# A 33rd head of zeros, one copy of 594 columns for each key and query tile, and a new instruction list

## The chip, the cores and the metric

The kernel runs on one core of one Trainium2 chip. The metric is the device time of one execution in microseconds; a profiled execution also gives a trace, whose span runs from the first to the last instruction. The engines are named as the profile names them: PE (TensorE, matmul), DVE (VectorE), ACT (ScalarE), POOL (GpSimd), and SP, whose queue issues nearly all DMAs.

## What is computed

One transformer block over 2048 tokens of width 576 with 32 heads of 18, and a feed-forward layer of width 4608. Its first half is a linear attention whose feature map is a pair of softmaxes:

```python
h = layernorm(x) * (1 + ca) + sa             # ca, sa: from silu(c) @ w_mod
q, k, v = split(h @ wqkv)                    # 32 heads of 18
pq, pk = q @ w_phi, k @ w_phi                # per head, 18 x 18
phi_q = concat(softmax(pq), softmax(-pq))    # 36 features per head
phi_k = concat(softmax(pk), softmax(-pk))
o = phi_q @ (phi_k^T v) / (phi_q @ sum(phi_k) + 1e-6)
x = x + ga * (o @ wo)
h = layernorm(x) * (1 + cb) + sb
x = x + gb * (relu(h @ w1) @ w2)
```

## The kernel before

**Tiling.** The 2048 tokens are 16 tiles of 128 rows, four tiles to a block. Channels are five chunks (KC = 5) of 128, 128, 128, 128 and 64 rows. The weights of keys and queries are folded with w_phi and with the modulation ahead of use (`wfold`), so that one projection gives the feature inputs of a tile. A projection of a tile is ten matmuls: five chunks for each of two PSUM banks. Heads lie in groups of three (GH = 3, GF = 54 columns); 32 heads make ten full groups and one of two heads, and the buffers have room for eleven full groups (DP = 594). Before the change a key or query tile fills 270 columns of the first bank and 306 of the second (`PARTS`), and leaves PSUM in two copies (`features`): 540 columns for the ten full groups and 36 for the two heads of the last. POOL has set the missing head's columns to zero beforehand (`pad_keys`, `queries_out`).

**Order.** Everything up to the second block of the feed-forward layer is written out by hand as a list of steps (`order`), and each engine runs its instructions strictly in the order of that list; POOL's alone are placed by the framework. The steps that matter here, a number after the name being the tile, pair or chunk:

- LP, LK, LA, LV, LQ, WOL, LW, W2: DMAs of x, key weights, modulation weights, value weights, turned query weights, wo, w1 and w2.
- LS (statistics of one tile of x), RS (its reciprocal deviation, on ACT, for two tiles), LX (normalise two tiles, on DVE), PT and PX (turn two tiles on PE and copy them out) or LT (turn one by DMA).
- WT (turn a chunk of the key weights on PE), WTE (copy it out), F1 and F0 (fold a chunk of keys or queries with w_phi), FA and FB (copy out its two banks).
- SIL (silu of c), MC1.0 and MC1.1 (shift and scale on PE), MSH and MSC (copy them out), SC1, SCv, SC0 (scale the folded weights), Bv, B1, B0 (their bias rows on PE), BEv, BE1, BE0 (copy these out).
- V, K, Q (project a tile), VE, KE, QE (copy it out).
- MN, LO, MX, HI, EX, SU, SA, RC, SC: the softmaxes of the keys (smallest and largest, subtract, exp, sums on PE, their copy, reciprocal, scale); SD takes the sums on DVE instead of SU and SA. The same with q in front is for two tiles of queries; qT turns them by DMA.
- KVa to KVc (keys times values on PE), KVE (copy out), NU and NUE (attention of the first two tiles and its division), OT and OTE, WS (scale wo by its gate on DVE), WO and WOE (output projection, residual), then S2, R2, X2, PN, PNE (second norm) and G.0, the first group of the feed-forward layer.

A last 1 moves a step from its usual engine to the other: KE, VE and QE are on ACT unless so marked, LS, WTE, FA, FB, PX, SC, BE and KVE are on DVE unless so marked. Tiles of PSUM for folds, projections and turned weights come from one pool of three (`mm_tile`), so a step that opens a tile waits until the third one before it has been copied out.

**Statistics.** On DVE a tile takes two `bn_stats` and a `bn_aggr` (L234, L235). On ACT (L228 to L230) it takes two passes over the tile with a running sum; what these passes write out is not used, and goes to `junk`.

**The buffer `room`.** Several short-lived tensors share one buffer of 12760 columns and are told apart by columns alone. `part(o, k, n)` gives k times n columns from column o:

```python
wv_raw, wqT, wq_plain = part(0, KC, D), part(3552, NGR, D), part(7008, KC, D)
junk = room[:, 9944:9944 + D]
```

So `wq_plain`, the folded query weights, ends at column 7008 + 5 x 576 = 9888. `zero_rows` lets POOL set the unused lower 64 partitions of the fifth chunk to zero in `wk_plain`, `wv_raw`, `wfold[1]`, `wv_sb`, then in `v`, then in `wq_plain` and `wfold[0]`. The framework makes an instruction wait for earlier ones that touch the same bytes of a buffer.

Of the kernel before, what the change touches and what calls it, by code (L numbers as in the profile page):

```python
# [44 lines left out]
def kernel(  # L45
# [41 lines left out]
    def copy(eng, dst, src):  # L87
        if eng is A_:
            A_.activation(out=dst, in_=src, func=ACT.Copy)  # L89
        else:  # L90
            eng.tensor_copy(out=dst, in_=src)
# [254 lines left out]
    def fold(which, ci):  # L346
        ps = pool_tiles["F", which, ci] = mm_tile("ps_fold")
        for g in range(NGR):
            nf = G6 if g < 5 else 2 * DH
            T_.matmul(ps[0:KK[ci], g // 4, (g % 4) * G6:(g % 4) * G6 + nf], lhsT=wT[which][0:G6, g, ci * P:ci * P + KK[ci]],  # L350
                      rhs=wbd[0:G6, g, 0:nf], start=True, stop=True)
# [93 lines left out]
    def proj(pss, lhs, w, splits):  # L445

        for ps, (cs, cn) in zip(pss, splits):
            for ci in range(KC):
                T_.matmul(ps[:, 0:cn], lhsT=lhs[:, ci, :], rhs=w[:, ci, cs:cs + cn],  # L449
                          start=(ci == 0), stop=(ci == KC - 1))  # L450
# [479 lines left out]
    LX.2 K.0 LS.8 PM.3 PM.0 K.2 LS.11 KE.2.1 VE.1 RS.3 KE.0 LQ.4 K.1 LX.3 LQ.0 LS.10.1 KE.1 LQ.3 K.3 KE.3 F0.4  # L930
    FB0.4.1 FA0.4.1 LT.5 V.5 LS.9 RS.4 LT.4 F0.2 VE.5 K.5 MN.0 FA0.2.1 FB0.2.1 F0.1 LO.1 KE.5 FB0.1.1 LT.6 RS.5
    FA0.1 CR LX.4 SC0.4 LT.7 V.4 VE.4 LP4.6 LX.5 F0.0 FB0.0.1 FA0.0.1 SC0.1 MX.0 SC0.2.1 K.6 KE.6 F0.3 FB0.3.1
    FA0.3.1 K.4 KE.4 LT.10 K.7 B0 LS.13 KE.7 BE0.1.1 LS.12.1 K.10 SC0.0 KE.10 RS.6 LT.9 LT.8 BE0.0 SC0.3 Q.1
    HI.1 Q.2 LS.14.1 QE.2 Q.0 LO.0 LM.1 LM.0 LT.11 HI.0 QE.1.1 V.9 QE.0 LS.15.1 VE.9 K.9 LM.2 KE.9 EX.0 Q.3 Q.7
    QE.3 RS.7 V.7 VE.7 MN.1 qMX.0 MX.1 qHI.0 LX.6 SU.0 EX.1 QE.7.1 LO.2 K.8 KE.8 K.11 KE.11 LT.12 LT.13 HI.2
    SU.1 LX.7 EX.2 qMN.0 qLO.0 K.12 KE.12 LO.3 SA.1 RC.1 qEX.0 RW.1 HI.3 RW.0 RWE.0.1 V.8 RWE.1 V.13 SA.0 LT.14
    VE.8 RC.0 LT.15 K.15 RC2.0 K.14 VE.13 qEX.1 MN.2 KE.15 MX.2 W1 KE.14 qSU.0 K.13 EX.3 RC2.1 LW.2.1 KE.13 Q.4
    QE.4 SU.3 V.15 LW.1.0 Q.8 LO.5 SC.0 qSA.0 HI.5 LO.4 RC2.2 HI.4 EX.4 LW.1.1 SC.1 SA.3 RC.3 VE.15 LW.0.0 qRC.0
    V.6 MN.3 QE.8 MX.3 SU.2 RD.2 RD.0 LW.0.1 LO.7 VE.6 SA.2 EX.5 SU.4 Q.14 SA.4 HI.7 SC.3 RC.2 SC.2 Q.13 V.14
# [5 lines left out]
    RL.4 W2.1.1 G.2 FW.7 qMN.2 qT.1 NV.0 qLO.2 qHI.2 NVE.0 RL.6 Y.1.0.0 RL.7 Y.1.1.0 qEX.4 Y.1.1.1 qEX.5 qSD.5
    qSD.4 FW.8 NV.1 qRC.2 OU.0 Y.1.0.1 RL.8 NVE.1 qSC.2 WP.0 Y.0.0.0 WPE.0 S3.0 W2.2.1 Y.1.0.2 YE.1.0 OU.1 WP.1
    WPE.1 S3.1 Y.1.1.2 YE.1.1 R3 X3 XT qT.2 MD.0 MD.3 Y.0.0.1 Y.0.0.2 Y.0.1.0 MD.1 MD.2 Y.0.1.1 YE.0.0 MD.4
    Y.0.1.2 YE.0.1
# [104 lines left out]
```

## Time and profile before

| what | us |
|---|---|
| median of 3 runs (414.61 to 415.11) | 415.0 |
| the profiled execution's own time | 417.61 |
| its span | 415.4 |
| first projection of a tile starts at | 18.04 |
| last keys times values start at | 88.70 |
| feed-forward layer (G.0) starts at | 103.79 |

The profile's groups give the busy time of a kind of instruction, its mean length in ns, and the idle time of its engine just ahead of it with what ended that idle time. A timeline row has the start, the length of the stretch, the engine, the line, the output and inputs with their shapes, a count, and in square brackets the idle time before it. An engine starts an instruction before the one ahead has left it, so rows can overlap, and the distance between starts is what an instruction costs its engine.

### The profile page before, as it was taken

What the parts mean: (1) busy time and instruction counts of PE and PEld (TensorE: products, weight loads), DVE (VectorE), ACT (ScalarE), POOL (GpSimd) and SP (SyncE); (2) the same over time, 40 slices, a digit from 0 to 9 for tenths busy, and PEclk for the clock granted to TensorE, in tenths of its full rate; (3) what the DMA queues carried; (4) which work ended last, traced back from release to release, by engine and by line L of the source; (5) the groups of instructions that cost most, each with busy time, mean ns of one, the idle gap of its engine ahead of it and who ended that gap; (6) DMA issues with size and microseconds to landing.
All of it is one profiled execution on the core that took longest, in us unless ns stands there. A gap on an engine that the chain in (4) does not pass through costs nothing.

```text
span 415.4 us, 9230 instructions
## 1 busy us (share of the span) xinstructions
PE 405.5 (98%) x3955; PEld 330.0 (79%) x3955; DVE 235.2 (57%) x597; ACT 182.7 (44%) x310; POOL 11.6 (3%) x39
## 2 busy tenths in 40 slices
PE   6999999989999999999999999999999999999996
PEld 4677777777888788788878888888888888878876
DVE  6789999977768564637345552846292532330011
ACT  7898999944761064016302630452055014302500
POOL 8010000000000000000000000000000000000000
PEclk9899999999999999999999999999999999999999
DMA  8955937489543520502051014104210502010000
GB/s 239 254 88 143 250 50 232 58 227 390 203 87 101 120 45 2 115 16 33 15 102 32 17 33 85 46 2 74 58 34 2 117 24 25 16 32 16 2 2 28
DMA packets 72163, 35.44 MB, mean 85 GB/s; under 512 B 56689, under 2 KB 69754, under 8 KB 72122
## 3 DMA queue, kind: packets, MB, share of 16 engines
q1 hardware_dynamic: 71520, 34.83, 35.3%
q8 instruction: 31, 0.51, 0.5%
q10 hardware_dynamic: 602, 0.02, 0.1%
q14 instruction: 10, 0.08, 0.1%
HBM read 19.27 MB, written 2.37 MB: 52 GB/s over the span
## 4 chain that ended last, share of the span: by engine, by line
PE 78%; DVE 12%; ACT 4%; DMA 2%; issue 2%; SPq 1%; DVEq 0%; ACTq 0%
PE ps_y L860 34%; PE ps_h L817 31%; PE ps_h L809 4%; PE ps_wo L725 3%; DVE tree L468 2%; PE ps_wo L449 2%; DVE tree L466 1%; DMA wo_sb<-in_A_wo_dram 1%; DVE xn L243 1%; DVE phik L481 1%; DMA wk_raw<-in_A_wqkv_dram 1%; DVE phik L479 1%; DVE phik L539 1%; ACT v L89 1%; PE ps_num L668 1%
## 5 line engine op out<-in xcount | busy, mean ns | idle before, releaser
L822 ACT ACTIVATE H<-ps_h 128x1024 bf16<-128x1024 f32 x72 | 73.5, 1022 | 170.8 <-PE ps_h L809 122.3
L860 PE MATMUL ps_y<-w_sb,H 128*128 128x288 bf16 (+2 forms) x1188 | 143.0, 282 | 0.0
L860 PEld LDWEIGHTS <-H 128*128 128x128 bf16 x1188 | 113.7, 98 | 27.3
L817 PE MATMUL ps_h<-hT,w1a 128*128 128x256 bf16 x640 | 74.9, 273 | 0.2 <-DVE hT L419 0.2
L817 PEld LDWEIGHTS <-w1a 128*128 128x128 bf16 x640 | 61.3, 98 | 9.6 <-issue 2.1
L868 DVE TENSOR_TENSOR outt<-ps_y,row_gb 128x288 bf16<-128x288 f32 (+2 forms) x33 | 14.8, 449 | 86.4 <-PE ps_y L860 86.2
L817 PE MATMUL ps_h<-hT,w1b 128*128 128x256 bf16 x512 | 59.2, 273 | 0.0
L449 PEld LDWEIGHTS <-hT 128*128 128x128 bf16 x480 | 46.0, 97 | 13.0 <-issue 0.9
L817 PEld LDWEIGHTS <-w1b 128*128 128x128 bf16 x512 | 49.8, 98 | 6.8 <-issue 0.8
L730 DVE TENSOR_TENSOR x_sb<-x_sb,ps_wo 128x288 bf16<-128x288 bf16 x28 | 12.6, 454 | 31.3 <-PE ps_wo L725 24.8
L243 DVE TENSOR_SCALAR xn<-x_sb,mv,rstd 128x576 bf16<-128x576 bf16 x32 | 12.5, 432 | 20.1 <-ACT rstd L239 20.1
L449 PE MATMUL ps_q<-wfold,hT 128*128 128x270 bf16 (+1 forms) x160 | 21.5, 285 | 0.1
L449 PE MATMUL ps_v<-wv_sb,hT 128*128 128x288 bf16 x160 | 21.2, 286 | 0.2 <-ACT phik L89 0.2
L449 PE MATMUL ps_k<-wfold,hT 128*128 128x270 bf16 (+1 forms) x160 | 21.3, 285 | 0.0
L526 DVE TENSOR_REDUCE ln_s<-room 128x66 f32<-128x1188 bf16 x14 | 19.0, 1367 | 2.6 <-ACT room L508 2.6
L809 PE MATMUL ps_h<-hT,w1c 64*128 64x256 bf16 x288 | 19.9, 271 | 0.0
L234 DVE BATCH_NORM_STATS2 bst<-x_sb 128x6 f32<-128x288 bf16 x48 | 19.4, 447 | 0.0
L508 ACT ACTIVATE room<-room 128x1188 bf16<-128x1188 bf16 x16 | 18.8, 1186 | 0.8 <-DVE room L479 0.3
L508 ACT ACTIVATE phik<-phik 128x2376 bf16<-128x2376 bf16 x8 | 17.5, 2193 | 0.3 <-DVE phik L481 0.2
L809 PEld LDWEIGHTS <-w1c 64*128 64x128 bf16 x288 | 12.1, 94 | 5.2 <-issue 3.8
L468 DVE TENSOR_TENSOR tree<-tree 128x264 bf16<-128x264 bf16 (+2 forms) x48 | 14.6, 305 | 1.7
L419 DVE TENSOR_SCALAR hT<-hT,mod 128x256 bf16<-128x256 bf16 x35 | 9.7, 344 | 6.2 <-DMA hT<-xn 6.2
(155 smaller groups left out, 362.1 us busy)
## 6 DMA issues: line engine op xcount, KB each, us to landing
w_sb<-in_B_w_dram SPq DMA_DIRECT2D x6, 864.0 KB, 10.5
...
```

Source lines behind the costliest of these rows:

```text
L234: V.bn_stats(out=st[:, half, :], in_=x_sb[:, t0 + j, half * 288:(half + 1) * 288])
L243: V.tensor_scalar(out=xn[:, j, 0:D], in0=x_sb[:, t0 + j, :], scalar1=mv[:, j, 0:1], scalar2=rs[:, j:j + 1], op0=ALU.add if j in minus else ...
L449: T_.matmul(ps[:, 0:cn], lhsT=lhs[:, ci, :], rhs=w[:, ci, cs:cs + cn], start=(ci == 0), stop=(ci == KC - 1))
L468: V.tensor_tensor(out=a[:, :, 0:w], in0=a[:, :, 0:w], in1=a[:, :, w:2 * w], op=op)
L508: A_.activation(out=E[:, j:j + k], in_=E[:, j:j + k], func=ACT.Exp)
L526: V.tensor_reduce(out=t["l", b][:, k * 22:(k + 1) * 22].rearrange("p (g s) h -> p g s h", s=2), op=ALU.add, axis=mybir.AxisListType.X, in_ ...
L730: V.tensor_tensor(out=xs[:, cs:cs + cn], in0=xs[:, cs:cs + cn], in1=p[:, 0:cn], op=ALU.add)
L809: T_.matmul(f1[q][:, e, hh * w:hh * w + w], lhsT=w1["c"][r, 2 * q + hh, :], rhs=hT[r, 4, :], start=(first and hh == 0), stop=(not first an ...
L817: T_.matmul(f1[q][:, e, hh * w:hh * w + w], lhsT=w1_at(2 * q + hh, e, ci), rhs=hT[:, ci, :], start=(first and hh == 0 and ci == 0), stop=( ...
L822: A_.activation(out=p2t["H1"].rearrange("p (e j) n -> p e j n", e=2)[:, :, 2 * q:2 * q + 2], in_=f1[q][:].rearrange("p e (h n) -> p e h n" ...
L860: T_.matmul(ps[:, 0, 0:cn], lhsT=p2t["H1"][:, k, j * P:(j + 1) * P], rhs=p2t["w2"][:, k, c], start=(k == 0), stop=(k == NJ - 1))
L868: V.tensor_tensor(out=o[:, c], in0=ps[:, 0, 0:cn], in1=rows["gb"][:, c], op=ALU.mult)
```

## The change

1. `wfold`, `wk_plain` and `wq_plain` get 594 columns instead of 576. The last group of the fold has three heads, the third of them made of zeros (`feature_maps`, `fold`).
2. A key or query tile fills 297 columns at the end of the first bank and 297 at the start of the second, which lie side by side, and leaves PSUM in one copy of 594 columns. The zeros of the missing head come out of the projection, and POOL no longer writes them.
3. The list of steps is a new one. In it ACT takes the statistics of five tiles (0, 1, 5, 14, 15) instead of eight (2, 3, 1, 6, 10, 12, 14, 15), and steps change place and engine throughout.

```diff
-    wfold = {i: wqp.tile([P, KC, D], BF16, name=f"wfold{i}") for i in (0, 1)}
+    wfold = {i: wqp.tile([P, KC, DP], BF16, name=f"wfold{i}") for i in (0, 1)}
...
-    wv_raw, wqT, wq_plain = part(0, KC, D), part(3552, NGR, D), part(7008, KC, D)
+    wv_raw, wqT, wq_plain = part(0, KC, D), part(3552, NGR, D), part(7008, KC, DP)
...
-    wplain = {1: p0.tile([P, KC, D], BF16, name="wk_plain"), 0: wq_plain}
+    wplain = {1: p0.tile([P, KC, DP], BF16, name="wk_plain"), 0: wq_plain}
...
-        for g, c, h, nh in ((slice(0, 5), 0, 0, 3), (slice(0, 5), GF, 3, 3), (slice(5, 6), 0, 0, 2)):
+        for g, c, h, nh in ((slice(0, 5), 0, 0, 3), (slice(0, 5), GF, 3, 3), (slice(5, 6), 0, 0, 3)):
...
-            nf = G6 if g < 5 else 2 * DH
+            nf = G6 if g < 5 else GF
...
-        c0, n = ((0, 432), (432, 144))[half]
+        c0, n = ((0, 432), (432, DP - 432))[half]
...
+    PH = DP // 2
+    PARTS = [(0, PH), (PH, PH)]
...
-    PARTS = [(0, 5 * GF), (5 * GF, D - 5 * GF)]
...
     def pad_keys(b):
-        G.memset(phik_g(b)[:, :, NG - 1, 0:GF], 0.0)
         G.memset(phik[b][:, TPB * NG * DW:], 0.0)
...
-        proj((ps[:, 0], ps[:, 1]), hT1[b][:, :, j * P:(j + 1) * P], w, HALVES if name == "v" else PARTS)
+        proj((ps[:, 0], ps[:, 1]) if name == "v" else (ps[:, 0, 512 - PH:], ps[:, 1]), hT1[b][:, :, j * P:(j + 1) * P], w, HALVES if name == "v" else PARTS)
...
     def features(dst, ps, eng):
-        copy(eng, dst[:, 0:10, :].rearrange("p (a g) c -> p a g c", a=2),
-             ps[:, :, 0:5 * GF].rearrange("p a (g c) -> p a g c", c=GF))
-        copy(eng, dst[:, 10, :].rearrange("p (f h) -> p f h", h=GH)[:, :, 0:2],
-             ps[:, 1, 5 * GF:5 * GF + 36].rearrange("p (f h) -> p f h", h=2))
+        copy(eng, dst, ps[:].rearrange("p a n -> p (a n)")[:, 512 - PH:512 + PH].rearrange("p (g c) -> p g c", c=GF))
...
     def queries_out(t, eng):
         b, j = t // TPB, t % TPB
-        if b not in pq_zero:
-            pq_zero.add(b)
-            G.memset(pq[b][:, :, NG - 1, :], 0.0)
...
     order = """
-    LP.1 LH WBD LS.3.1 LK.2 WT.4 WTE.4 LK.0 WT.0 LK.1 LS.2.1 WTE.0 WT.1 WTE.1 F1.4 FB1.4 LP.0 LS.0 Z.11 RS.1
-    LX.1 FA1.4.1 F1.1 Z.8 LA.1 SIL WT.3 WTE.3 WT.2 LA.0 LS.1.1 Z.3 FB1.1.1 FA1.1.1 F1.0 RS.0 WTE.2.1 FB1.0 FA1.0
-    PT.1 LX.0 F1.3 F1.2 FA1.3 PX.1.1.1 MC1.0 PX.1.0.1 FB1.3.1 MSH LV MC1.1 FB1.2 MSC SCv.3 SCv.0 PT.0 PX.0.1
...
-    RC.6 SC.5 SU.7 Q.10 QE.10 KVa qT.0 SA.7 SC.6 WOL RC.7 SC.7 WS.1 VE.12 KVb KVc Q.12 KVE.0.1 RD.1 KVE.1 NU.1
+    LH LP.0 LS.0.1 LP.1 LK.1 WT.3 LS.3 LS.1.1 LS.2 LK.0 WBD WTE.3 Z.6 WT.0 WTE.0 WT.2 RS.1 LX.1 WT.1 WTE.1
+    WTE.2.1 F1.0 FA1.0 LK.2 LA.0 SIL RS.0 FB1.0.1 WT.4 LA.1 PT.1 PX.1.1 F1.1 WTE.4.1 FA1.1 FB1.1 LV LP4.2
+    PX.1.0.1 F1.2 MC1.0 FA1.2.1 FB1.2.1 CR F1.3 FA1.3.1 LX.0 LQ.2 F1.4 FB1.4 MC1.1 MSH MSC SCv.0 SCv.1 FA1.4.1
+    FB1.3.1 SCv.3 PT.0 SCv.2.1 Bv PX.0.1.1 PX.0.0 BEv.1.1 BEv.0.1 B1 BE1.1.1 SC1.0.1 BE1.0.1 LQ.3 LQ.4 LP4.4
...
+    qMX.1 WOL LW.1.0 RC.3 RC.2 HI.5 VE.4 LO.7 HI.7 RD.0 qSU.0 qSA.0 SC.1 V.15 SC.2 MCE2 LO.6 HI.6 QE.12 V.11
...
+    SC.4 SU.6 SA.6 RC.6 VE.14 SC.5 SU.7 SA.7 SC.6 KVa KVb RC.7 SC.7 KVc WS.1 KVE.0.1 Q.4 QE.4 KVE.1 WS.0 NU.1
+    NUE.1 Q.6 NU.0 OT.1 QE.6 OTE.1 NUE.0 Q.9 QE.9 OT.0 OTE.0 qMN.1 WO.1 WOE.1 S2.1 WO.0 WOE.0 S2.0 R2 Q.15 Q.5
...
     """
```

With `wq_plain` of 594 columns a chunk, that tensor ends at column 7008 + 5 x 594 = 9978 of `room`; `junk` still begins at 9944.

More of the change, by code (lines that the diff above doesn't have):

```diff
@@ L363, in fold_scale @@
             V.tensor_scalar_mul(d, f, m)
+    PH = DP // 2
+    PARTS = [(0, PH), (PH, PH)]
     def fold_bias(which, src):
+        w = D // 2 if which == "v" else PH
         ps = pool_tiles["B", which] = mm_tile("ps_bias")
@@ L370, in fold_bias @@
                 p = 64 - half * 64
-                T_.matmul(ps[p:p + 1, half, 0:288], lhsT=sal[:, ci:ci + 1], rhs=src[:, ci, half * 288:(half + 1) * 288],
+                T_.matmul(ps[p:p + 1, half, 0:w], lhsT=sal[:, ci:ci + 1], rhs=src[:, ci, half * w:(half + 1) * w],
                           start=(ci == 0), stop=(ci == KC - 1))
     def fold_bias_out(which, dst, half, eng):
-        p = 64 - half * 64
-        copy(eng, dst[64:65, 4, half * 288:(half + 1) * 288], pool_tiles["B", which][p:p + 1, half, 0:288])
+        p, w = 64 - half * 64, D // 2 if which == "v" else PH
+        copy(eng, dst[64:65, 4, half * w:(half + 1) * w], pool_tiles["B", which][p:p + 1, half, 0:w])
     rows = {}
@@ L566 @@
           [const.tile([P, TPB, DP], BF16, name="pq0")[:]] + [part(b * TPB * DP, TPB, DP) for b in range(3)]]
-    pss, pq_zero = {}, set()
+    pss = {}
     def project(name, t, w):
@@ L924 @@
     order = """
-    LP.1 LH WBD LS.3.1 LK.2 WT.4 WTE.4 LK.0 WT.0 LK.1 LS.2.1 WTE.0 WT.1 WTE.1 F1.4 FB1.4 LP.0 LS.0 Z.11 RS.1
-    LX.1 FA1.4.1 F1.1 Z.8 LA.1 SIL WT.3 WTE.3 WT.2 LA.0 LS.1.1 Z.3 FB1.1.1 FA1.1.1 F1.0 RS.0 WTE.2.1 FB1.0 FA1.0
-    PT.1 LX.0 F1.3 F1.2 FA1.3 PX.1.1.1 MC1.0 PX.1.0.1 FB1.3.1 MSH LV MC1.1 FB1.2 MSC SCv.3 SCv.0 PT.0 PX.0.1
-    LP4.2 FA1.2.1 LQ.5 SCv.2.1 Bv B1 SCv.1.1 PX.0.0 LQ.1 BEv.0.1 BE1.1.1 SCv.4 BEv.1 BE1.0.1 SC1.1 LQ.2 LP4.4
-    V.2 SC1.0 LS.4 LS.5 V.3 SC1.4.1 V.0 VE.2 SC1.2.1 SC1.3.1 VE.0.1 OPEN LS.7 PM.2 VE.3 V.1 RS.2 LS.6.1 PM.1
@@ L930 @@
[L930 to L939, printed above, removed]
@@ L940 @@
-    LO.6 EX.7 QE.14 SU.5 HI.6 qSC.0 RC.4 V.11 VE.14 SA.5 QE.13 EX.6 SC.4 V.10 V.12 RC.5 VE.11 VE.10 SD.12 SD.13
-    RC.6 SC.5 SU.7 Q.10 QE.10 KVa qT.0 SA.7 SC.6 WOL RC.7 SC.7 WS.1 VE.12 KVb KVc Q.12 KVE.0.1 RD.1 KVE.1 NU.1
-    WS.0 NUE.1 Q.9 QE.12 QE.9 NU.0 OT.1 Q.6 OTE.1 LW.2.0 NUE.0 qMN.1 QE.6 OT.0 WO.1 WOE.1 S2.1 OTE.0 WO.0 Q.11
-    QE.11 WOE.0 Q.15 Q.5 P2 W2.0.1 MCE2 S2.0 R2 QE.5 QE.15 W2.0.0 X2 PN PNE G.0 FW.1 RL.0 qMX.1 qHI.1 qLO.1
-    qEX.2 qSD.2 qEX.3 qSD.3 qMX.2 RL.1 FW.2 RL.2 G.1 RL.3 qRC.1 LW.3.1 LW.3.0 FW.5 RL.5 W2.1.0 W2.2.0 qSC.1 FW.4
@@ L945 @@
[L945 to L948, printed above, removed]
+    LH LP.0 LS.0.1 LP.1 LK.1 WT.3 LS.3 LS.1.1 LS.2 LK.0 WBD WTE.3 Z.6 WT.0 WTE.0 WT.2 RS.1 LX.1 WT.1 WTE.1
+    WTE.2.1 F1.0 FA1.0 LK.2 LA.0 SIL RS.0 FB1.0.1 WT.4 LA.1 PT.1 PX.1.1 F1.1 WTE.4.1 FA1.1 FB1.1 LV LP4.2
@@ new lines @@
+    PX.1.0.1 F1.2 MC1.0 FA1.2.1 FB1.2.1 CR F1.3 FA1.3.1 LX.0 LQ.2 F1.4 FB1.4 MC1.1 MSH MSC SCv.0 SCv.1 FA1.4.1
+    FB1.3.1 SCv.3 PT.0 SCv.2.1 Bv PX.0.1.1 PX.0.0 BEv.1.1 BEv.0.1 B1 BE1.1.1 SC1.0.1 BE1.0.1 LQ.3 LQ.4 LP4.4
+    SCv.4 LS.6 LS.7 SC1.1 SC1.4 V.3 VE.3 LQ.1 SC1.2.1 RS.3 V.1 VE.1 SC1.3 V.0 LX.3 K.0 LQ.5 VE.0.1 OPEN LQ.0
+    LS.5.1 K.3 LS.4 LT.6 LS.8 RS.2 KE.0 LX.2 LS.9 KE.3 LS.10 LS.11 K.1 KE.1 K.2 KE.2 F0.3 FB0.3.1 F0.0 LT.4
+    FA0.3.1 FB0.0.1 FA0.0.1 RS.4 K.6 SC0.0 KE.6 F0.1 FB0.1.1 V.2 LT.7 FA0.1.1 MX.0 RS.5 F0.2 FB0.2.1 VE.2 K.7
@@ new lines @@
+    FA0.2.1 SC0.3.1 LX.4 LT.5 LP4.6 LX.5 KE.7 MN.0 SC0.2 LO.0 SC0.1 LM.0 F0.4 FA0.4.1 FB0.4.1 LT.11 K.5 KE.5 B0
+    SC0.4 BE0.1.1 BE0.0.1 LS.12 K.4 LS.15.1 PM.2 V.5 VE.5.1 LO.1 KE.4 PM.3 LS.13 LT.10 LT.9 Q.1 LS.14.1 QE.1 Q.7
+    LT.8 MN.1 K.9 K.11 QE.7 Q.3 LO.2 HI.0 KE.9 RS.6 KE.11 LM.1 QE.3 EX.0 Q.0 QE.0 LM.2 RS.7 K.8 LX.6 MX.1 HI.1
+    Q.2 LX.7 LT.14 KE.8 SU.0 QE.2 LT.15 HI.2 RW.0 RW.1 RWE.0.1 RWE.1.1 qMX.0 K.10 EX.2 LO.3 Q.8 qMN.0 KE.10 K.14
+    QE.8 qHI.0 KE.14 qLO.0 MN.2 qEX.1 V.9 LO.4 V.7 LO.5 VE.9 W1 RC2.0 LT.13 LT.12 K.13 RC2.2 VE.7 EX.1 V.6 V.12
@@ new lines @@
+    SA.0 HI.3 RC2.1 MX.2 HI.4 LW.2.0 KE.13 PM.1 RD.2 SU.2 SD.2 SD.3 VE.6 RC.0 EX.3 VE.12 K.15 KE.15 K.12 qEX.0
+    KE.12 V.8 VE.8 SC.0 V.10 SA.2 MX.3 SU.3 PM.0 RC.1 VE.10 MN.3 Q.10 EX.4 Q.13 QE.10 V.4 QE.13 SA.3 LW.1.1 Q.12
+    qMX.1 WOL LW.1.0 RC.3 RC.2 HI.5 VE.4 LO.7 HI.7 RD.0 qSU.0 qSA.0 SC.1 V.15 SC.2 MCE2 LO.6 HI.6 QE.12 V.11
+    EX.5 V.13 SC.3 SU.4 SU.5 VE.11.1 qRC.0 EX.7 VE.15 SA.5 EX.6 V.14 Q.14 VE.13 SA.4 RC.4 RC.5 QE.14 qSC.0 qT.0
+    SC.4 SU.6 SA.6 RC.6 VE.14 SC.5 SU.7 SA.7 SC.6 KVa KVb RC.7 SC.7 KVc WS.1 KVE.0.1 Q.4 QE.4 KVE.1 WS.0 NU.1
@@ new lines @@
+    NUE.1 Q.6 NU.0 OT.1 QE.6 OTE.1 NUE.0 Q.9 QE.9 OT.0 OTE.0 qMN.1 WO.1 WOE.1 S2.1 WO.0 WOE.0 S2.0 R2 Q.15 Q.5
+    QE.15 Q.11 P2 W2.1.0 LW.0.0 LW.0.1 LW.2.1 X2 PN PNE QE.5 qLO.1 qHI.1 QE.11 W2.2.0 qEX.3 qSD.3 LW.3.0 LW.3.1
+    qEX.2 G.0 FW.1 RL.0 W2.1.1 qSD.2 qMX.2 qHI.2 FW.2 RL.1 qRC.1 RL.2 G.1 W2.2.1 RL.3 FW.4 qSC.1 RL.4 W2.0.1
+    qT.1 W2.0.0 FW.5 RL.5 G.2 RL.6 qMN.2 NV.0 NVE.0 FW.7 NV.1 RL.7 qLO.2 qEX.5 FW.8 qEX.4 NVE.1 OU.0 RL.8
+    Y.1.0.0 WP.0 WPE.0 Y.0.0.0 S3.0 RD.1 OU.1 Y.1.0.1 WP.1 Y.0.0.1 qSD.4 WPE.1 S3.1 qSD.5 Y.1.0.2 YE.1.0 R3 X3
@@ L949 @@
+    XT MD.2 MD.0 qRC.2 qSC.2 Y.0.0.2 YE.0.0 MD.4 MD.1 Y.0.1.0 Y.0.1.1 MD.3 Y.1.1.0 Y.0.1.2 qT.2 Y.1.1.1 Y.1.1.2
+    YE.1.1 YE.0.1
     """
```

## The prediction

> **What bounds the kernel now.** I read the page first, then the busy time by stage, then whom PE waited for, then the timelines of the start and of the hand-over to the feed-forward layer. The page and the stages (columns: stretch, its length, then busy time with count of PE, PEld, DVE, ACT, POOL, the granted clock, DMA share, GB/s):
>
> ```profile
> span 415.4 us, 9230 instructions
> ...
> PE 405.5 (98%) x3955; PEld 330.0 (79%) x3955; DVE 235.2 (57%) x597; ACT 182.7 (44%) x310; POOL 11.6 (3%) x39
> ```
>
> ```profile
> 0.00:18.00 18.00, 13.50 (x159) 9.97 (x159) 13.16 (x44) 13.24 (x32) 9.05 (x27) 0.91 1.00 239
> 18.00:84.00 66.00, 65.65 (x581) 50.76 (x580) 61.50 (x134) 62.65 (x136) 2.50 (x12) 1.00 0.62 143
> 84.00:104.00 20.00, 18.15 (x304) 15.00 (x300) 15.61 (x38) 9.54 (x27) 0.00 (x0) 1.00 0.98 318
> ```
>
> PE is busy for 98% of the span, and a busy PE need not be PE at its peak. Whether it is shows in the distance between starts and in what it waited for from 18 to 104:
>
> ```profile
> 18.04 5.07 PE L449 MATMUL ps_v<-wv_sb,hT 128*128 128x288 bf16 x40
> 22.95 5.07 PE L449 MATMUL ps_k<-wfold,hT 128*128 128x270 bf16 x40
> ```
>
> ```profile
> PE ps_num L668 <- DVE KVZ L641: 1.2, 1, 1.2
> PE ps_kv L627 <- DVE phik L539: 0.3, 1, 0.3
> PE ps_v L449 <- ACT phik L89: 0.2, 1, 0.2
> PE ps_h L817 <- DVE hT L419: 0.2, 1, 0.2
> ```
>
> Forty matmuls of 288 columns take 22.95 - 18.04 = 4.91 us, 123 ns each, and they follow each other without a hole. Of 86 us PE waited 1.9 in sight, 1.2 of them in one place. ACT (62.65 of 66) and DVE (61.50 of 66) are nearly full too, but they are just fast enough. So the end is set by three things: when the first projection starts (18.04), how much PE has to do after it, and the few holes. A lighter ACT alone gains nothing from 18 to 84, for all its holes there that stop PE are the 0.2.
>
> **The copies and the statistics.** What ACT saves (timeline):
>
> ```profile
> 3.76 0.68 ACT L228 ACTIVATE room<-x_sb 128x576 bf16<-128x576 bf16 x1 [1.74 <-DMA x_sb<-in_A_x_dram]
> ...
> 7.65 0.30 ACT L238 ACTIVATE rstd<-mv,eps_t 128x2 f32<-128x2 f32 x1
> ...
> 25.43 0.72 ACT L89 ACTIVATE phik<-ps_k 128x540 bf16<-128x540 f32 x2
> ...
> 27.85 1.30 ACT L89 ACTIVATE phik<-ps_k 128x540 bf16<-128x540 f32 x4
> ```
>
> ```profile
> L234 DVE BATCH_NORM_STATS2 bst<-x_sb 128x6 f32<-128x288 bf16 x48 | 19.4, 447 | 0.0
> ...
> L89 ACT ACTIVATE v<-ps_v 128x576 bf16<-128x576 f32 x15 | 9.5, 640 | 0.2 <-PE ps_v L449 0.2
> ```
>
> (Groups: busy us, mean ns of one, idle time before.) One pair lasts 0.72, two 1.30, so a pair costs ACT 0.58; one copy of 576 lasts 0.64 and, two to three per cent longer, one of 594 some 0.66. It saves 0.06 in length and less in occupation: 29 pairs, at most 2 us. Three tiles fewer of statistics save 3 x 1.95 (two tiles take 3.76 to 7.65) = 5.8. DVE takes these three tiles, about 1.0 each (two halves of 447 ns, and the rest small), gives up three key or query copies and takes two more of values: about +0.7 between the modulation and the last scaling. None of this is on PE's path, for the reason above; it costs 1 to 3 us if DVE falls behind PE, and gains at most PE's waits for them, 0.3 + 0.2.
>
> **PE's added columns.** A chunk of a key or query tile had 270 + 306 columns and gets 2 x 297, 18 more:
>
> ```profile
> L449 PE MATMUL ps_k<-wfold,hT 128*128 128x306 bf16 x80 | 13.0, 292 | 0.0
> ...
> L449 PE MATMUL ps_k<-wfold,hT 128*128 128x270 bf16 x80 | 11.8, 278 | 0.0
> ```
>
> 36 columns are 14 ns, so 18 are 7; times 5 chunks and 32 tiles that is **+1.1 us**, all on PE's path, which has no cover.
>
> **The start.** This is where I expect most of the time to go. In the new list ACT's first compute step is the statistics of tile 0. They write `junk`, columns 9944 to 10520 of `room`; `wq_plain` now reaches 9978, and POOL zeroes its fifth chunk. So this first step must wait for that memset, which it didn't touch before (9888). The rows of POOL and ACT (beside the two of ACT above), of DVE and of PE:
>
> ```profile
> 7.84 0.58 POOL L191 MEMSET room<- 64x576 bf16 x1
> ...
> 7.98 0.20 ACT L239 ACTIVATE rstd<-rstd 128x2 f32<-128x2 f32 x1
> ...
> 11.71 0.79 ACT L89 ACTIVATE wT<-ps_wT 108x768 bf16<-108x768 bf16 x1
> 12.40 1.29 ACT L89 ACTIVATE hT<-psT_h 128x512 bf16<-128x512 bf16 x2
> ```
>
> ```profile
> 10.21 0.16 DVE L306 TENSOR_SCALAR sg<-sg 128x5 f32<-128x5 f32 x1
> ...
> 10.71 0.55 DVE L91 COPY wT<-ps_wT 108x768 bf16<-108x768 bf16 x1
> ...
> 12.51 0.76 DVE L243 TENSOR_SCALAR xn<-x_sb,mv,rstd 128x576 bf16<-128x576 bf16 x2
> 13.19 0.60 DVE L91 CAST wk_plain<-ps_fold 128x432 bf16<-128x432 f32 x1
> ```
>
> ```profile
> 11.31 0.42 PE L350 MATMUL ps_fold<-room,wT 108*128 108x108 bf16 x6 [0.16 <-DVE wT L91]
> 11.58 0.72 PE L267 MATMUL psT_h<-ident,xn 128*128 128x128 bf16 x10
> ...
> 13.20 1.39 PE L318 MATMUL ps_mod<-siluc,wma 128*128 128x1 bf16 x50
> ```
>
> The memset ends at 8.42, so ACT starts at 8.45 instead of 3.76, 4.7 late, with everything of ACT queued behind it. Both tiles of statistics (3.89): 12.3. RS.1 (0.5): 12.9. WTE.2 (0.79): 13.7. WT.4 needs the PSUM tile that WTE.2 empties, so PE stands before it from the end of F1.0, which I put at about 9.5, until 13.7. Meanwhile DVE, in the new order, has LX.1 ahead of WTE.1, and LX.1 waits for RS.1: 12.9 + 0.76 = 13.65, WTE.1 14.2, FA1.0 14.8, the silu (10.21 to 10.71, 0.5 to 0.6) 15.4. PE: WT.4, PT.1 15.2, F1.1 and F1.2 16.1, MC1.0 (half of 1.39) 16.8, F1.3 (after PX.1.0 on ACT, which ends at 16.2) and F1.4 17.7, MC1.1 18.4. Before, the modulation ended at 14.59, and from there to the first projection it was 18.04 - 14.59 = 3.45, with PT.0, Bv and B1 between, as in the new list. 18.4 + 3.45 = 21.85. The granted clock (fourth figure) was low in that stretch:
>
> ```profile
> 14.50:17.90 3.40, 3.40 (x34) 0.50 1.49 129
> ```
>
> At full clock PE's part of it would be shorter, but copies of ACT and DVE lie in between; I take 21.7. **Start: +3.65**, bounds +1.9 (all 3.45 halved by the clock) and +4.7 (all of ACT's delay).
>
> The row says that a stretch of 3.4 us ran at half clock, the stretch from 11 to 14.5 with its holes lying ahead of it. The Trainium skill, "TensorE: Matmul & The Clock Gate", Part 1: The HAM clock gate, says that activity in a free-running window of about 3.4 us decides the clock of what follows, and that a gap of more than that throttles it again. The trace agrees with one such window. By that rule the hole before WT.4 (9.5 to 13.7) throttles the same window as before, and one more if the small matmuls from 13.7 on don't count as busy; the third rival below prices that from rows.
>
> **The hand-over.** Before, wo was loaded late:
>
> ```profile
> 84.51 0.58 SPq L184 DMA_DIRECT2D wo_sb<-in_A_wo_dram  x1
> ...
> 88.70 0.80 PE L627 MATMUL ps_kv<-v,phik 128*128 128x57 bf16 x22 [0.29 <-DVE phik L539]
> ...
> 90.84 1.06 DVE L413 TENSOR_TENSOR wo_sb<-wo_sb,row_ga 128x1728 bf16<-128x1728 bf16 x1 [2.20 <-DMA wo_sb<-in_A_wo_dram]
> ...
> 92.14 0.28 PE L668 MATMUL ps_num<-KVZ,ET 108*128 108x57 bf16 x3 [1.18 <-DVE KVZ L641]
> ...
> 103.79 1.92 PE L817 MATMUL ps_h<-hT,w1a 128*128 128x256 bf16 x16 [0.16 <-DVE hT L419]
> ```
>
> On DVE the scaling of wo stood ahead of the copy of KVZ and waited 2.2 for the DMA, which stood in SP's queue behind the two transposes of qT.0; PE lost 1.2 to it. The new list issues wo ahead of qT.0, by some ten steps of DVE, and puts Q.4 ahead of NU.1. So that hole closes: **-1.3**, bounds -2.2 (all of DVE's wait) and 0 (another wait in its place). What is late next: w1c is now loaded after the first piece of w2, behind qT.0; it is wanted 1.9 us into G.0, 16.2 us after the keys are summed (88.70 + 0.80) and still 14.9 with the hole closed, and so has time. Six Q tiles stay in this stretch, whose columns are counted above. From G.0 on the work of PE is the same, and the last w2 load now stands behind qT.1: 0, bounds -0.3 and +1.5.
>
> **The middle.** PE may lose less there than its 0.5 of waits, as ACT has room, or more, if DVE, which leaves the start 4 late, holds it; against that DVE had a hole of its own that shrinks when V starts later than its statistics:
>
> ```profile
> DVE v L91 <- PE ps_v L449: 1.8, 1, 1.8
> ```
>
> I take -0.6, bounds -1.4 (1.8 + 0.3 less the 0.7 above) and +1.5.
>
> **Sum**, against the profiled span of 415.4: 1.1 + 3.65 - 1.3 - 0.6 = +2.85, so a span of 418.25. The span stands 0.4 above the median of the runs (415.0; the profiled execution's own time was 417.61, the profile's cost), so the forecast is 415.0 + 2.9 = **417.9**.
>
> **Rivals.**
>
> - *ACT isn't held* (0.10): POOL's spans are rough, and the memset may be done when x lands, at 3.76. Then by the steps above each of ACT's ends is 4.2 to 4.7 earlier, V starts at about 17.5, and the sum is 1.1 - 0.5 - 1.3 - 0.6 = -1.3: 413.7, faster. The point is V's start: from 18.0 down the kernel is faster. Against it: the row puts the memset 4 us behind that.
> - *ACT was the bound* (0.05): the 5.8 + 2 us taken from ACT shorten the stage from 18 to 84, as the change says. ACT's 62.65 of 66 speaks for it, PE's single wait of 0.2 for ACT against it. Half of it would give 417.9 - 3.9 = 414.0.
> - *Half clock for one more window* (0.17): PE's hole at the start lets the clock fall, and the first 3.4 us of projections run at 0.50, 1.7 us more: 419.6. For it: the row of 14.50 to 17.90 followed a stretch that was not full. Against it: by 21.7 PE has been working for 8 us.
>
> The forecast has 0.68, with a range of its own from 416.2 to 419.6.
>
> **Numbers.** The range for 8 in 10 goes from 415.4 (start at its lower bound, hand-over and middle kind) to 419.8 (the third rival). A measurement of this kernel tells about 0.2%, 0.8 us, from no change. Faster: most of the first rival, some of the second, 0.10; same: the remainder of these and the low end of the forecast, 0.09; slower 0.81.
>
> **What would show it.** ACT's first L228 starts at about 8.5 and waits for POOL; WT.4 and the value projections start near 13.7 and 21.7; L449 has one width of 297 for keys and queries; the row with 2.20 on wo is gone and PE's wait for KVZ with it; G.0 starts near 106.6. I am wrong if V starts by 18, if PE shows new waits for DVE of over 1 us between V and the last keys, or if the stretch from the keys' end to G.0 still takes 14.3.

## The result and the profile after

The changed kernel takes 425.25 us (median of four runs, 422.24 to 426.80), the kernel before 415.06 beside it: a ratio of 1.0232, 95% interval 1.0209 to 1.0254. It is slower, as predicted, but by 10.2 us and not by 2.9, and far outside the range. The profiled execution took 426.66.

The page's head, and four stretches of it (columns as in the prediction):

```profile
span 424.5 us, 9157 instructions
...
PE 409.3 (96%) x3953; PEld 332.1 (78%) x3953; DVE 234.1 (55%) x598; ACT 178.7 (42%) x271; POOL 9.9 (2%) x31
```

```profile
22.40:62.00 39.60, 38.95 (x350) 29.13 (x349) 33.97 (x91) 34.09 (x72) 0.81 (x5) 1.00 0.49 125
62.00:65.00 3.00, 0.36 (x3) 0.06 (x1) 2.97 (x6) 2.84 (x3) 0.46 (x1) 1.00 0.30 59
65.00:68.80 3.80, 3.77 (x18) 2.35 (x19) 3.63 (x7) 0.79 (x2) 0.00 (x0) 0.56 0.40 43
68.80:113.40 44.60, 44.25 (x510) 35.14 (x509) 36.52 (x72) 30.91 (x50) 0.00 (x0) 1.00 0.57 170
```

PE still does nearly all of the chain of work that ended last (91% of the span), and it is still full in the first and the last of these stretches. Between them there is something that the kernel before doesn't have: 3 us in which PE has 0.36 of work, and behind them 3.8 us at a mean clock of 0.56.

The timeline of the start, with the first value projection:

```profile
7.85 0.59 POOL L191 MEMSET room<- 64x594 bf16 x1
...
8.48 0.68 ACT L228 ACTIVATE room<-x_sb 128x576 bf16<-128x576 bf16 x1 [6.47 <-DMA wma<-in_w_mod_dram]
...
12.78 0.77 DVE L243 TENSOR_SCALAR xn<-x_sb,mv,rstd 128x576 bf16<-128x576 bf16 x2 [4.38 <-ACT rstd L239]
...
13.50 0.80 PE L340 MATMUL ps_wT<-ident,wk_raw 128*108 128x128 bf16 x6 [3.92 <-ACT wT L89]
```

```profile
22.46 4.83 PE L453 MATMUL ps_v<-wv_sb,hT 128*128 128x288 bf16 x30
```

ACT's first statistics start when POOL's memset of `wq_plain` ends (7.85 + 0.59 = 8.44), and the chain runs from there as predicted: statistics, RS.1, DVE's LX.1, and WT.4 at 13.50. (The row names a DMA as what ended ACT's wait; experiment 5 has the same instruction with POOL named.) V starts at 22.46.

The hole in the middle: what PE and SP's queue waited for, then the timeline of DVE, ACT, SP and PE there.

```profile
PE ps_k L453 <- DMA hT<-xn: 2.7, 1, 2.7
PE ps_k L453 <- ACT pq L89: 0.4, 1, 0.4
```

```profile
SPq L399 <- ACT room L511: 5.2, 1, 5.2
```

```profile
48.74 0.76 DVE L243 TENSOR_SCALAR xn<-x_sb,mv,rstd 128x576 bf16<-128x576 bf16 x2
...
60.51 1.19 ACT L511 ACTIVATE room<-room 128x1188 bf16<-128x1188 bf16 x1
...
61.76 0.60 SPq L399 DMA_DIRECT2D mods_d<-room  x1
62.41 2.52 SPq L258 DMA_TRANSPOSE hT<-xn  x2
...
65.03 2.28 PE L453 MATMUL ps_k<-wfold,hT 128*128 128x297 bf16 x10 [2.67 <-DMA hT<-xn]
```

K.13 wants a transposed tile of x. In the new list LT.13 and LT.12 stand behind RC2.0, the write of `mods_d`, on SP's queue. That write waits until ACT's qEX.1 is done (60.51 + 1.19 = 61.70), and the two transposes, whose rows DVE had normalised by 48.74 + 0.76 = 49.50, wait behind it. In the old list LT.14 and LT.15, the last two, stand ahead of RC2.0, and in the trace of before the last four transposes leave ahead of the write:

```profile
49.77 6.10 SPq L258 DMA_TRANSPOSE hT<-xn  x4
58.66 0.60 SPq L395 DMA_DIRECT2D mods_d<-room  x1
```

The last keys times values and G.0:

```profile
95.02 5.23 PE L623 MATMUL ps_kv<-v,phik 128*128 128x57 bf16 x176
...
113.38 1.91 PE L813 MATMUL ps_h<-hT,w1a 128*128 128x256 bf16 x16 [0.25 <-DVE hT L423]
```

From the end of the one to the start of the other it is 13.13, against 14.29 in the trace of before.

### The profile page after: what moved, and what is told of

It reads as the page before. It is cut to its first block, busy times and chain, and to the rows that moved or that the text cites. A ratio compares the mean times of both kernels' runs of the same rounds, so it can differ in the third digit from the quotient of the medians.

```text
span 424.5 us, 9157 instructions
## 1 busy us (share of the span) xinstructions
PE 409.3 (96%) x3953; PEld 332.1 (78%) x3953; DVE 234.1 (55%) x598; ACT 178.7 (42%) x271; POOL 9.9 (2%) x31
## 4 chain that ended last, share of the span: by engine, by line
PE 91%; ACT 3%; DMA 2%; DVE 2%; issue 1%; SPq 0%
PE ps_y L856 33%; PE ps_h L813 30%; PE ps_h L805 4%; PE ps_v L453 4%; PE ps_q L453 4%; PE ps_k L453 4%; PE ps_wo L721 3%; PE ps_sum L518 2%; PE ps_wo L453 2%; PE ps_kv L623 1%; DMA wma<-in_w_mod_dram 1%; PE ps_num L664 1%; DMA x_sb<-in_A_x_dram 1%; ACT room L228 1%; ACT room L230 1%; DMA hT<-xn 1%
## 5 line engine op out<-in xcount | busy, mean ns | idle before, releaser
L453 PEld LDWEIGHTS <-hT 128*128 128x128 bf16 x480 | 47.2, 100 | 19.3 <-DMA hT<-xn 3.0
L726 DVE TENSOR_TENSOR x_sb<-x_sb,ps_wo 128x288 bf16<-128x288 bf16 x28 | 12.7, 455 | 34.4 <-PE ps_wo L721 24.8
L453 PE MATMUL ps_k<-wfold,hT 128*128 128x297 bf16 x160 | 23.2, 298 | 3.3 <-DMA hT<-xn 2.7
L453 PE MATMUL ps_v<-wv_sb,hT 128*128 128x288 bf16 x160 | 22.9, 302 | 0.0
L234 DVE BATCH_NORM_STATS2 bst<-x_sb 128x6 f32<-128x288 bf16 x54 | 21.7, 443 | 1.2 <-DMA x_sb<-in_A_x_dram 1.1
L453 PE MATMUL ps_q<-wfold,hT 128*128 128x297 bf16 x160 | 22.1, 290 | 0.0
## 6 DMA issues: line engine op xcount, KB each, us to landing
w_sb<-in_B_w_dram SPq DMA_DIRECT2D x6, 864.0 KB, 11.7
```

The lines of the kernel that those rows point to most:

```text
L234: V.bn_stats(out=st[:, half, :], in_=x_sb[:, t0 + j, half * 288:(half + 1) * 288])
L726: V.tensor_tensor(out=xs[:, cs:cs + cn], in0=xs[:, cs:cs + cn], in1=p[:, 0:cn], op=ALU.add)
```

## The experiments

Each was run in five rounds beside the kernel before (415.05 to 415.25 in all of them).

**1. Junk moved.** In the changed kernel:

```
-    junk = room[:, 9944:9944 + D]
+    junk = room[:, 9984:9984 + D]
```

> The changed kernel with junk moved to columns 9984 to 10560 of room, so that the statistics on ScalarE no longer share columns with wq_plain; nothing else is different. Theory of two separate waits: ACT's first statistics start near 3.8 instead of 8.48, the first value projection near 18 instead of 22.46, at full clock; the hole of 2.7 us ahead of K.13, and the half-clock window behind it, stay, since they come from the order on SP's queue. That is 425.25 less 4.4 and less 0.96 of half clock: about 420. Rival, one cause for all: the hole at 62 is only the late start seen further down, and goes with it: about 415.5. Rival, the list is what costs: moving junk gives less than 2 us: over 423.

Measured: 419.47 (ratio 1.0090, 1.0071 to 1.0109). The theory of two separate waits. ACT and the first projection, what PE waited for, and the stretches around the hole:

```profile
3.70 0.68 ACT L228 ACTIVATE room<-x_sb 128x576 bf16<-128x576 bf16 x1 [1.69 <-DMA x_sb<-in_A_x_dram]
```

```profile
16.85 3.84 PE L453 MATMUL ps_v<-wv_sb,hT 128*128 128x288 bf16 x30 [0.50 <-DVE wv_sb L363]
```

```profile
PE ps_k L453 <- DMA hT<-xn: 2.7, 1, 2.7
```

```profile
54.90:58.80 3.90, 1.23 (x11) 0.77 (x9) 3.80 (x7) 2.85 (x3) 0.47 (x1) 1.00 0.43 85
58.80:62.10 3.30, 3.30 (x16) 2.09 (x15) 3.20 (x6) 0.76 (x2) 0.00 (x0) 0.50 0.31 16
```

ACT starts 4.8 earlier and V at 16.85, but the hole has the same 2.7 and the half clock stands behind it: the late start didn't cause them. Four of the six runs have a mean clock of 0.995 or 0.996 and took 419.5 to 419.7; the two with 1.000 took 417.8 and 418.3.

**2. Transposes first.** In the changed kernel's list:

```
-    ... LO.3 Q.8 qMN.0 KE.10 K.14
+    ... LO.3 Q.8 LT.13 LT.12 qMN.0 KE.10 K.14
...
-    ... VE.9 W1 RC2.0 LT.13 LT.12 K.13 ...
+    ... VE.9 W1 RC2.0 K.13 ...
```

> The changed kernel with the two steps LT.13 and LT.12 ahead of RC2.0 in the list instead of behind it, so that on SP's queue the two transposes don't stand behind the write of mods_d, which waited 5.2 us for ACT. Theory of two separate waits: the hole of 2.7 ahead of K.13 goes, and with it the half clock of the 3.4 us behind it (1.7 us): 425.25 less 4.4, about 421. Rival, one cause for all: the K tiles are late for another reason (their normalised rows come late), and the hole stays at over 2 us: about 425. Rival, the clock falls anyway: only the 2.7 go, about 422.5.

Measured: 422.19 (1.0163, 1.0145 to 1.0182). What PE waited for from 22 to 109:

```profile
PE ps_k L453 <- ACT pq L89: 0.4, 1, 0.4
PE ps_h L813 <- DVE hT L423: 0.3, 1, 0.3
PE ps_k L453 <- ACT phik L89: 0.2, 1, 0.2
```

The hole is gone, and behind V's first matmuls (thirty of them take 4.70, against 3.84 in experiment 1) the clock stays at full. The time lies between the two expectations for that: 3.1 less than the changed kernel, of which 2.7 are the hole.

**3. Both edits.**

> Both edits together: junk at columns 9984 to 10560, and LT.13 and LT.12 ahead of RC2.0. Theory of two separate waits: what is left of the change is PE's added columns (+1.1), the hand-over (-1.15 measured in the changed kernel's trace) and some tenths in the middle and at the end, so 414.5 to 416, the kernel before within 0.3%. Rival, the list or the longer copies cost something else: 417 or more, with new waits of PE in the middle.

Measured: 414.82 (0.9989, 0.9979 to 1.0000), as the theory had it. PE's waits from 16 to 102:

```profile
PE ps_v L453 <- DVE wv_sb L363: 0.5, 1, 0.5
PE ps_h L813 <- DVE hT L423: 0.3, 1, 0.3
PE ps_k L453 <- ACT phik L89: 0.2, 1, 0.2
```

So all of the loss is in these two places. Against 414.82 the shared columns alone cost 7.4 (experiment 2), the order on SP's queue alone 4.65 (experiment 1), both together 10.4. In the medians the two don't add up (12.0 against 10.4, or 10.9 and 11.1 by experiments 13 and 14); in the spans of the four traces they do: 420.2 - 413.3 = 6.9 and 417.4 - 413.3 = 4.1, together 11.0 against 424.5 - 413.3 = 11.2.

**4. Parts 1 and 2 of the change with the old list**, junk at 9984.

> Parts 1 and 2 of the change alone (594 columns, one copy for a key or query tile, zeros from the projection) with the list of the kernel before, and junk at columns 9984 to 10560. My sum: PE's added columns +1.1, nothing else on PE's path: 416.2. Rival, ACT's shorter occupation is worth something: 415 or less. Rival, the one longer copy releases its PSUM tile later and stalls PE: over 417.

Measured: 415.17 (0.9997, 0.9988 to 1.0006). No difference from before; my 416.2 is missed, and the rival's 415 fits better. What PE waited for from 16 to 102:

```profile
PE ps_v L453 <- ACT phik L89: 0.3, 1, 0.3
PE ps_h L813 <- DVE hT L423: 0.2, 1, 0.2
```

**5. The kernel before with 34 shared columns.**

```
-    junk = room[:, 9944:9944 + D]
+    junk = room[:, 9854:9854 + D]
```

> The kernel before with junk at columns 9854 to 10430 of room, so that it shares its first 34 columns with wq_plain, as in the changed kernel; nothing else is different. Theory: the shared columns are what costs at the start, whatever the list: ACT's first statistics wait for POOL's memset (8.4 instead of 3.8), PE then stands in the start and stays at half clock until some 24 us: V starts 5 to 6 later, 420 to 422. Rival, the old list doesn't mind (other work of ACT first, or DVE turns the weights): under 417. Rival, only the wait of 4.7 is added, at full clock: 418 to 419.5.

Measured: 421.92 (1.0162, 1.0138 to 1.0186), 6.7 above the kernel before and as the theory had it. One number changed in the kernel before gives the loss of the start:

```profile
8.45 0.68 ACT L228 ACTIVATE room<-x_sb 128x576 bf16<-128x576 bf16 x1 [6.44 <-POOL room L191]
...
13.33 0.72 PE L340 MATMUL ps_wT<-ident,wk_raw 128*108 128x128 bf16 x6 [3.14 <-ACT wk_plain L89]
```

```profile
22.83 2.41 PE L449 MATMUL ps_v<-wv_sb,hT 128*128 128x288 bf16 x15
```

So either list pays for the shared columns: with the old one V comes 6.4 later than in experiment 8 (22.83 against 16.42), with the new one 5.6 later than in experiment 1 (22.46 against 16.85). The move also lays 90 columns of `junk` over the buffer of the queries' softmaxes (columns 7128 to 9944), which the expectation left out; from V to G.0 this trace takes 85.37 against 84.76 in experiment 8, so that costs little, if anything.

**6. Fills in the start's hole**, on top of experiment 2, whose columns are still shared:

```
+    "ZZ": fill,
...
-    ... FB1.0.1 WT.4 LA.1 ...
+    ... FB1.0.1 ZZ.11 WT.4 LA.1 ...
```

> As the kernel with LT.13 and LT.12 first (422.19, junk still shared), with eleven matmuls of zeros, 512 columns each, put between F1.0 and WT.4, so that PE works through the hole of 4.2 us while ACT waits; their results go nowhere. Theory, the wait and the cold clock cost separately: the fills don't move WT.4 much (13.5), but from there PE runs at full clock; the stretch from WT.4 to V takes 6.8 as with junk moved instead of 9.0, and V's first matmuls lose nothing: 422.19 less 2.2 less 1.0 = 419. Rival, the stretch hangs on the copies of ACT and DVE: only the 1.0 of V's own matmuls comes back, 421.2. Rival, fills only delay WT.4: 422 or more.

Measured: 419.52 (1.0098, 1.0077 to 1.0119), 2.7 less than without fills. PE:

```profile
9.71 2.93 PE L207 MATMUL ps_warm<-zeros 128*128 128x512 bf16 x11
13.52 0.49 PE L340 MATMUL ps_wT<-ident,wk_raw 128*108 128x128 bf16 x6 [0.88 <-ACT wT L89]
```

```profile
20.23 3.83 PE L453 MATMUL ps_v<-wv_sb,hT 128*128 128x288 bf16 x30 [0.50 <-DVE wv_sb L363]
```

WT.4 starts where it did, but from there to V it is 6.7 instead of 8.96, and the six matmuls of WT.4 take 0.49 instead of 0.80. So of the 7.4 that the shared columns cost, 2.7 are the clock of PE, and 4.7 stay with the fills in. The traces put this rest at 3.8 (spans of 417.1 and, in experiment 3, 413.3): V starts 3.3 later (20.23 against 16.95), as ACT is held, and from V to G.0 it is 0.6 longer, for which no single wait stands out.

**7. The list alone**: 576 columns, two copies, junk not shared, the new list with the transposes first.

> The list alone: the kernel before (576 columns, two copies for a key or query tile, zeros from POOL, junk not shared) with the new list, LT.13 and LT.12 first and the steps PM right behind OPEN, where they stand in the old one. Against both edits together (414.82) it tells the columns apart under the new list. My sum: PE has 1.1 less to do, 413.7. Rival, as the old list with 594 columns showed no difference (415.17 against 415.11), the shorter copies pay for the columns: 414.8. Rival, two copies a tile hold ACT up under the new list: 415.5 or more.

Measured: 415.15 (0.9994, 0.9981 to 1.0007). The 413.7 of the sum is missed; nearest is the second expectation. The list by itself, without its place for LT.13 and LT.12, is worth nothing either way.

**8. The kernel before, unchanged.**

> The kernel before, unchanged, for a second trace. Its first trace belongs to an execution of 417.61, above all its other runs (414.6 to 416.5), with a stretch of half clock from 14.5 to 17.9. Theory: a usual execution has none there, V starts near 16.5 instead of 18.04 and the span is about 413; then my start term was too small by about 1.5, as it was counted from 18.04. Rival: the trace is usual, V starts at 18.0 and the profile itself adds 2.5. Open as well: whether the 1.2 us that PE waits ahead of the attention of the first tiles are there again.

Measured: 415.13; the profiled execution took 414.83, among its other runs (414.71 to 415.73).

```profile
16.42 5.07 PE L449 MATMUL ps_v<-wv_sb,hT 128*128 128x288 bf16 x40
```

```profile
87.39 0.80 PE L627 MATMUL ps_kv<-v,phik 128*128 128x57 bf16 x22 [0.29 <-DVE phik L539]
...
89.25 0.56 PE L668 MATMUL ps_num<-KVZ,ET 108*128 108x57 bf16 x11
...
101.18 1.92 PE L817 MATMUL ps_h<-hT,w1a 128*128 128x256 bf16 x16 [0.17 <-DVE hT L419]
```

V starts at 16.42, 1.6 earlier than in the trace that the prediction used, the attention of the first tiles has no wait ahead of it (DVE waits 0.8 for wo instead of 2.20), and G.0 starts at 101.18 instead of 103.79. The span is 412.8. The first trace was of an execution 2.5 us longer than usual. PE's waits from 16 to 102, to be set beside those of experiment 4:

```profile
PE ps_v L449 <- ACT phik L89: 0.5, 1, 0.5
PE ps_kv L627 <- DVE phik L539: 0.3, 1, 0.3
PE ps_h L817 <- DVE hT L419: 0.2, 1, 0.2
```

**9. The write of mods_d early**, on top of experiment 1; the transposes stay behind it:

```
-    ... RWE.0.1 RWE.1.1 qMX.0 ...
+    ... RWE.0.1 RWE.1.1 RC2.0 qMX.0 ...
...
-    ... VE.9 W1 RC2.0 LT.13 LT.12 K.13 ...
+    ... VE.9 W1 LT.13 LT.12 K.13 ...
```

> The kernel with junk moved (419.47, hole ahead of K.13 in it), with RC2.0, the write of mods_d, right behind RWE.1 in the list; the two transposes stay behind it. Theory: the write waited for ACT's exponential of the queries (qEX.1), which writes to the same buffer room ahead of it in the list and not to the row that is written out; from its new place it waits for RWE.1 alone, SP's queue is free some 5 us earlier, and the hole goes though the order of the three DMAs is the same: 414.8. Rival, the write waits for something else that is late (the row itself, POOL), or the transposes for their own rows: the hole stays, 419 or more.

Measured: 414.88 (0.9997, 0.9987 to 1.0007). SP's queue, and ACT around it:

```profile
49.84 0.60 SPq L399 DMA_DIRECT2D mods_d<-room  x1
50.49 2.97 SPq L258 DMA_TRANSPOSE hT<-xn  x2
```

```profile
49.31 0.41 ACT L89 ACTIVATE room<-ps_row 128x288 f32<-128x288 f32 x1 [0.20 <-PE ps_row L390]
...
53.01 0.67 ACT L89 ACTIVATE room<-ps_q 128x594 bf16<-128x594 f32 x1 [0.66 <-DMA mods_d<-room]
```

The write starts right behind the row that it reads (49.31 + 0.41 = 49.72), and the hole is gone with the queue's order unchanged. So in the changed kernel it waited for later work on other columns of `room`: in the kernel the row lies at columns 12176 to 12752, and qEX.1 works on 8536 to 9944. The last row shows the same from the other side: a copy of queries to other columns of `room` now waits 0.66 for the write. The rule given ahead of the prediction, that an instruction waits for earlier ones that touch the same bytes, doesn't cover these waits; why the row counts as shared with those columns wasn't tried and stays open.

**10. Fills in the middle's hole**, on top of experiment 1:

```
+        for _ in range(11 if (name, t) == ("k", 13) else 0):
+            T_.matmul(ps[:, 0], lhsT=ident[:], rhs=wfold[0][:, 0, 0:512], start=True, stop=True)
         proj(...)
```

> The kernel with junk moved (419.47), with eleven matmuls of 512 columns put into the hole ahead of K.13; they write to K.13's own PSUM tile, which its projection then overwrites. Theory: the hole keeps its 2.7 us, since the DMA ends it, but PE isn't throttled behind it, so the 1.7 us of the window at half clock come back: 417.8, with runs closer together than 417.8 to 419.7. Rival, the half clock has another cause than the hole: 419.5. Rival, the fills delay K.13: 420 or more.

Measured: 418.42 (1.0081, 1.0069 to 1.0093; 417.76 to 419.07), 0.6 above the theory.

```profile
54.60:57.50 2.90, 2.60 (x14) 1.02 (x12) 2.90 (x5) 2.74 (x3) 0.47 (x1) 1.00 0.32 63
57.50:61.00 3.50, 3.50 (x29) 2.76 (x30) 3.33 (x7) 1.55 (x4) 0.00 (x0) 1.00 0.36 44
```

K.13 comes no earlier, and the half clock behind it is gone, in all five runs by their mean clock (1.000). The medians differ by 1.05 and the intervals overlap, so its price is shown by the traces rather than by the times: from V to G.0 it is 89.32 in experiment 1 and 87.66 here, 1.7 less (the spans, 417.4 and 416.1, differ by 1.3). The runs lie 1.3 apart, against 1.9 in experiment 1, less of a gain than had been expected.

**11 and 12. Fills ahead of the first turn, and a scaling moved**, on top of experiment 3:

```
-    ... LK.1 WT.3 LS.3 ...
+    ... LK.1 ZZ.7 WT.3 LS.3 ...
```

```
-    ... PX.0.1.1 PX.0.0 ... LP4.4
-    SCv.4 LS.6 ...
+    ... PX.0.1.1 SCv.4 PX.0.0 ... LP4.4
+    LS.6 ...
```

> The kernel with both edits (414.82), with seven matmuls of zeros ahead of WT.3, in the 3.4 us in which PE waits for the first key weights. Theory: PE reaches full clock some 3.4 us earlier than 11.05, and the turns and folds from 7 to 11 take less: V starts 0.5 to 1.5 earlier, 413.3 to 414.3. Rival, that stretch hangs on DMAs and on the copies of ACT and DVE: 414.8.

> As the kernel before this one, and SCv.4 on DVE ahead of PX.0.0 instead of behind BE1.0, as V waited 0.5 for the fifth chunk of its weights. Theory: V starts up to 0.5 earlier than without that step's move. Rival, the bias row, which ACT writes into the same chunk, holds V just as long: no difference to the kernel with the fills alone.

Measured: 415.05 (0.9996, 0.9984 to 1.0008) and 415.44 (1.0007, 0.9998 to 1.0017). V starts 0.45 earlier (16.50) in the first, and no time comes of it. In the second V still waits as long, now for the bias row:

```profile
16.51 1.75 PE L453 MATMUL ps_v<-wv_sb,hT 128*128 128x288 bf16 x13 [0.50 <-ACT wv_sb L89]
```

**13 and 14. The changed kernel again, twice**, for its spread.

> The changed kernel, unchanged. Theory: the two causes add up except for the clock: the executions differ in whether PE runs at half clock behind the hole (1.7 us) and in when it first reaches full clock in the start (any time from V on, 3.4 us apart, 1.7 us); V starts 22.5 or about 1 to 2 earlier, the hole is always 2.5 to 2.9. Times between 422 and 427 in steps of about 1.7. Rival: the hole itself differs, from 0 to 2.8, with the DMAs around it.

> The changed kernel, unchanged, for a third trace, with the same expectations: V's start and its clock, the length of the hole ahead of K.13, and the clock behind it, each against the time of that execution.

Measured: 425.75 (423.79 to 426.42; ratio 1.0246, 1.0223 to 1.0270) and 425.94 (425.39 to 426.82; 1.0259, 1.0244 to 1.0274). From the first of the two:

```profile
12.70:22.40 9.70, 8.90 (x120) 7.16 (x119) 7.60 (x26) 6.65 (x17) 0.00 (x0) 0.50 0.97 217
...
61.50:64.00 2.50, 0.12 (x1) 0.00 (x0) 2.50 (x5) 2.34 (x2) 0.46 (x1) 0.99 0.34 67
64.00:67.40 3.40, 3.10 (x13) 1.94 (x14) 3.23 (x7) 0.79 (x2) 0.00 (x0) 0.51 0.34 49
```

In all three traces V starts at 22.46, PE waits 2.67 ahead of K.13, and the work behind this hole runs at half clock. Here the clock's record also covers the start: from 12.7 to V PE runs at 0.50. In the trace shown first it reads 1.00 there, but the matmuls have the length of half clock in both. What differs is how far half clock reaches into V and, by the mean clock of the runs, whether it follows the hole: two executions with a mean clock of 1.000 took 423.8 and 423.85, while 0.984 to 0.996 goes with 425.4 to 426.8. One run of 422.24 with 0.996 doesn't fit, and no trace shows it; the spread isn't wholly explained.

## Why the prediction was right in sign and wrong in size

From a usual execution before (experiment 8) to the trace after, the span grows by 424.5 - 412.8 = 11.7: V starts 22.46 - 16.42 = 6.04 later, from V to G.0 it is 90.92 instead of 84.76 (+6.16), and from G.0 to the end 311.12 instead of 311.62 (-0.5). The prediction's terms for these three are +3.65, 1.1 - 0.6 - 1.3 = -0.8, and 0.

- **What bounds the kernel: right.** PE from V to the end; ACT's lighter load gave nothing (experiments 4 and 7).
- **ACT is held: right**, to 0.2 us: 8.48 for 8.45, WT.4 at 13.50 for 13.7. Experiments 1 and 5 show it from both sides. The rival that ACT isn't held fell.
- **From WT.4 to V: mis-sized.** I took 8.0; it was 8.96 at half clock and is 6.7 at full clock. The third rival had the mechanism, but priced it with 1.7 for one window and gave it 0.17; by experiments 2 and 6 it costs 2.7, and it is there in every trace of the kernel, most of it ahead of V and not, as the rival had it, in V's own matmuls. My reason against it, that PE would have worked for 8 us by then, is what failed: PE worked, and the clock didn't rise.
- **The base of the start: wrong by 1.6.** I counted from 18.04, from an execution that had a window of half clock in its start, and put its 417.61 against the median of 415.0 down to the profile. Experiment 8 shows that the profile adds nothing: its execution took 414.83. Three numbers had said so beforehand: the execution's own time, the median and the row of 0.50.
- **The middle, -0.6: this is the step that failed most.** It weighed DVE and ACT, and left SP's queue out. The changed order there costs 2.67 at K.13 and, in three traces of three, half clock behind it (1.7 from V to G.0 between experiments 1 and 10): 4.4 of the 6.16, where the term stood at -0.6; some 1.0 more are V's first matmuls at half clock (4.83 against 3.84). I named new waits for DVE as what would make me wrong; the wait was for a DMA.
- **PE's added columns, +1.1: there, but paid for.** Thirty matmuls of queries ahead of the second norm take 112.18 - 108.36 = 3.82 in the trace after and 99.93 - 96.25 = 3.68 in experiment 8 (starts to starts of what follows), so the columns cost about 1.5 over 32 tiles. But experiments 4 and 7 differ from before by nothing that can be measured. The traces of experiments 8 and 4 show why: from V to G.0 PE's busy time rises from 83.45 to 84.24, and its idle time, in waits in sight and smaller gaps, falls from 1.31 to 0.55, so the stretch stays as long (84.76 and 84.79). The new list gives the same between experiments 7 and 3 (busy 83.29 and 84.25, idle 1.33 and 0.57). That the single copy closes these gaps, by freeing PSUM sooner, is argued, not shown. What failed here is the ground that was given, that the columns lie "all on PE's path, which has no cover".
- **The hand-over, -1.3: right in that one trace, not in a usual one.** The wait ahead of the attention is gone, but experiment 8 doesn't have it. From the keys' end to G.0 it is 13.13 after and, there, 12.99 (87.39 + 0.80 to 101.18).
- **After G.0, 0: right** within its bounds but for 0.2.

The repaired kernel (experiment 3) is 0.1% below the one before, with an interval that reaches 1.0000; no version here is faster than the kernel before by more than that.
